# Attention, a layer-normed MLP and a token-and-channel mixer on one core: the same instructions, with the SBUF tiles placed in another order

## The chip, the cores and the metric

The kernel runs on one core of a Trainium2 chip. The time is the device time of one launch in microseconds (us). Three runs of the kernel before took 1301.6, 1305.14 and 1305.99 us; the median is 1305.14 us.

## The reference

Three stages follow each other. B = 4 batches, H = 12 heads, S = 448 positions, D = 64 per head, C = 768 channels, all in float32:

```python
scores = cap * np.tanh((q @ k.T / 8) / cap)            # per batch and head, 448 x 448
attn   = softmax(scores, axis=-1)
x      = concat_heads(attn @ v)                        # (4, 448, 768)

xn = (x - mean) / np.sqrt(var + 1e-6) * g_ln
x  = x + np.maximum(xn @ w_ch1, 0) @ w_ch2             # 768 -> 3072 -> 768

h  = np.maximum(x.transpose(0, 2, 1) @ w_tok1, 0) @ w_tok2   # 448 -> 256 -> 448
u  = x + h.transpose(0, 2, 1)
out = u + np.maximum(u @ m2_w_ch1, 0) @ m2_w_ch2       # 768 -> 1536 -> 768
```

## The kernel before

Activations stay in SBUF with the channels on the partitions: a batch is six tiles of 128 channels by 448 positions. A large matrix product is done in float32r, in one pass of TensorE, and its accuracy is kept by splitting each operand into a high part and a low remainder (`low`, line 183): a product of two split operands is three matmuls (`PASSES`: high by high, low weight by high, high weight by low). Nearly every matmul so made reads 128 partitions by 128 columns as weights and then lets 128 by 448 move through them (128 by 384 in the first half of the token mixing).

The stages, by lines: attention of batches 0 and 1 with plain float32 matmuls (L467, L488), of batches 2 and 3 with split operands (L470, L513); the MLP layers of batches 0 and 1 (`mlp`: L1025 first layer, L998 second layer); token mixing (`tokens`: transposes L1059, products L1083 and L1108); for batches 2 and 3 the layers' products go through a seven-product (Strassen) form, all of whose matmuls are issued at L782. Weights come from HBM in 64-bit words, are put together on ScalarE and VectorE, split, and written back to HBM so that a later use only loads them. Attention of batches 2 and 3 runs beside the MLP of 0 and 1.

The order in which every engine gets its instructions is set by `Program.emit`, a list scheduler with a table of costs of its own. It runs while the kernel is built and knows nothing of addresses.

What concerns the change is where the tiles lie. All SBUF tiles come from one pool (`cp`) through `place` (line 173) and `boxes` (line 176). The pool hands out bytes of a partition in the order of the calls, and each tile begins at the next multiple of 32 bytes. The first tile, `kc`, begins at byte 16,512 of each partition and takes 704, so what follows begins at 17,216, which is 269 times 64. Which tiles a matmul reads as weights and which move:

- weights: `split0` to `split2` (weights of the layers), `whole` (whose room becomes `late_whole`, a fourth set), `t1` (first token matrix), `ks` and `vs` (keys and values of split attention), `pair_r`, `ones`;
- moving: `big0`, `big1` (normalised activations, split), `h0` to `h7` (hidden activations, split), `x0` to `x3`, `raw`, `own`, `two`, `qs`, `eh`, `el` and `t2`; the rooms of `x0`, `x1`, `raw`, `own` and `two` hold split operands too in the Strassen stages (`late_x`, `late_raw`, ...).

Within a tile the parts that a matmul reads begin at multiples of 512 bytes (weights; 640 in `vs`) or of 1792 and 1536 bytes (moving), which are all multiples of 64. So the place of a tile's first byte modulo 64 is that of every read from it.

Of the kernel before, what the change touches and what calls it, by code (L numbers as in the profile page):

```python
# [10 lines left out]
F32R = mybir.dt.float32r  # L11
I32 = mybir.dt.int32
U32 = mybir.dt.uint32
I64 = mybir.dt.int64
# [4 lines left out]
B, H, S, D = 4, 12, 448, 64  # L19
C = H * D  # L20
P = 128
NCC = C // P
# [3 lines left out]
G = 4  # L26
NG1, NG2 = NF1 // G, NF2 // G
NG = NG1 + NG2
DT = 256
NJ = S // 32  # L30
# [3 lines left out]
DV = D + 32  # L34
# [58 lines left out]
class Program:  # L93
# [12 lines left out]
    def add(self, engine, cols, run, reads=(), writes=(), early=0.0, lag=None, slack=0.0):  # L106

        names = [(name.strip("*+"), "*" in name, "+" in name) for name in engine.split("/")]  # L110
        costs = {e: self.FIXED[e] + self.RATE[e] * cols * (0.5 if half else 1.0) for e, half, _ in names}
        step = Step(costs, run, (self.key - early, len(self.steps)))
        step.port = {e for e, _, port in names if port}
        step.lag, step.slack = lag, slack
        before = set()
        for b in [p for b in reads for p in b.parts]:
            before.add(b.writer)
            b.readers.append(step)
        for b in [p for b in writes for p in b.parts]:
            before.add(b.writer)  # L120
            before.update(b.readers)
            b.writer, b.readers = step, []
        before -= {None, step}
        for s in before:
            s.users.append(step)
        step.waits = len(before)
        self.steps.append(step)
# [36 lines left out]
def block_kernel(ctx: ExitStack, tc: tile.TileContext, qkv, cap, gln, w1, w2, wt1, wt2, con, out):  # L164
# [10 lines left out]
    def place(name, shape, dtype=F32, tag=""):  # L175
        return cp.tile([P, *shape], dtype, name=name, tag=tag or name)

    def boxes(name, n, shape, dtype=F32):
        return [Box(place(f"{name}{i}", shape, dtype)) for i in range(n)]
# [11 lines left out]


    kc = place("kc", [K_PAIR])
    cap_t, tsc = place("cap_t", [1]), place("tsc", [1])
    gl = place("gl", [NCC])
    ones = place("ones", [P])
    pair_r = place("pair_r", [3, P], F32R)
    t1, t2 = place("t1", [2, 4 * DT], F32R), place("t2", [2, 2 * S], F32R)
    T1 = [Box(t1[:, :, i * 512:(i + 1) * 512]) for i in range(2)]
    T2 = [Box(t2[:, :, i * S:(i + 1) * S]) for i in range(2)]  # L200
    ident = kc[:, K_ID:K_ID + P]
    neg = kc[:, K_NEG:K_NEG + 1]

    raw_t, whole_t = place("raw", [2 * C], I64), place("whole", [2 * C], I32)
    RAW, WHOLE = [[Box(t[:, i * C:(i + 1) * C]) for i in range(2)] for t in (raw_t, whole_t)]
    split_t = [place(f"split{i}", [2, C], F32R) for i in range(3)]
    SPLIT = [[Box(t[:, :, :CC]), Box(t[:, :, CC:])] for t in split_t]
    x_t = [place(f"x{b}", [NCC, S]) for b in range(B)]
    X = [[Box(t[:, e]) for e in range(NCC)] for t in x_t]
    big_t = [place(f"big{i}", [NCC, 2, S], F32R) for i in range(2)]  # L210
    BIG = [[Box(t[:, e]) for e in range(NCC)] for t in big_t]
    HID = boxes("h", 2 * G, [2, S], F32R)


    own_t = place("own", [4, S])
    own = [Box(own_t[:, i]) for i in range(4)]
    own[2].parts = [Box(), Box()]
    OWN = [Box(own_t[:, 2 * i:2 * i + 2], own[2 * i:2 * i + 2]) for i in range(2)]
    QK = boxes("qk", 1, [S + 4 * P])
    QK[0].parts = [Box(QK[0].at[:, :S + 2 * P]), Box(QK[0].at[:, S + 2 * P:])]  # L220
    v_t, two_t = place("v", [4 * DV]), place("two", [2, S])
    V = [Box(v_t.rearrange("p (c d) -> p c d", c=4))]
    two = [Box(two_t[:, i]) for i in range(2)]
    SQ, SUM, OTHER = boxes("sq", 1, [S]), boxes("sum", 1, [S]), boxes("other", 1, [S])
    TWICE = [Box(OTHER[0].at[:, :CC].rearrange("p (e a d) -> p e a d", e=3, a=2), OTHER)]
    QS = boxes("qs", 1, [2, S], F32R)
    KS, VS = boxes("ks", 1, [4 * P], F32R), boxes("vs", 1, [4, DV + D], F32R)
    EH, EL = boxes("eh", 1, [2, S], F32R), boxes("el", 1, [2, S], F32R)
    M, N = boxes("m", 2, [2, 2, NJ]), boxes("n", 1, [2, 2, NJ])
    rs_t, rm_t = place("rs", [H, NJ]), place("rm", [H, NJ])  # L230
    RS = [Box(rs_t[:, 6 * g:6 * g + 6]) for g in range(2)]
    RM = [Box(rm_t[:, 6 * g:6 * g + 6]) for g in range(2)]
    R, VA = boxes("r", 1, [2, 32]), boxes("va", 1, [3, 8])
# [9 lines left out]
    def ring(of):  # L243
        while True:
            yield from of
# [6 lines left out]
    H11, H21, H4 = BIG[1][:2], [BIG[1][2], TWO], [*EH, *EL]  # L252
    H22, H1, H2, H3 = (HID[i:i + 2] for i in range(0, 8, 2))

    def relay():

        def later(old, boxes, fill):
            old = [p for box in old for p in box.parts]
            add("place", 0, fill, (), old + boxes)
# [9 lines left out]
        def fill_raw():  # L269
            t = place("late_raw", [3, 2, S], F32R, tag="raw")  # L270
            for i in range(3):
                X3[i].at = t[:, i]
            X4[2].at = QS[0].at

        later(RAW + QS, [*X3, X4[2]], fill_raw)

# [151 lines left out]
    def attention(b, start, pace):  # L428
# [8 lines left out]
        def head(h):  # L437
# [10 lines left out]
            if parted:  # L448

                (ks,), (qs,) = KS, QS  # L450
                add("act", 4 * P, lambda: act(ks.at, k, AF.Copy), [qk], [ks], early=PREPARE)  # L451
# [213 lines left out]

    HIDDEN = [ring(HID), ring(HID[:G]), ring(HID[G:])]
    PASSES = ((0, 0), (1, 0), (0, 1))
# [575 lines left out]
```

## Time and profile before

| | |
|---|---|
| median of 3 runs | 1305.14 us (1301.6 to 1305.99) |
| profiled execution: span from first to last instruction (the page gives no other time of it) | 1303.0 us |
| PE busy | 1289.0 us, 99%, 6171 matmuls |
| PE weight loads | 1115.8 us, 86%, 6171 |
| VectorE (DVE) busy | 1119.3 us, 86% |
| ScalarE (ACT) busy | 759.9 us, 58% |
| mean DMA rate | 210 GB/s |
| mean granted TensorE clock | 0.999 |

A matmul's busy time runs from its start to the end of its last result. Matmuls overlap, so the mean time of one (367 ns) is not the time from one to the next; the latter is read from a row that merges n matmuls of the chain of waits, by dividing its length by n. A float32 matmul that isn't a transpose stands as two records, a float32r matmul as one. All 6171 records that the program's matmuls should leave are there; 5597 of them are float32r, and of these 5412 move 448 columns in the lines L998, L1025, L782, L470, L513, L1108 and L574, and 176 move 384 columns in L1083.

### The profile page before, as it was taken

Reading aid. Unit: us, or ns where it says so; the run is one execution under the profiler, and the core shown is the slowest. Engines: PE = TensorE matmul, PEld = TensorE weight load, DVE = VectorE, ACT = ScalarE, POOL = GpSimd, SP = SyncE. Lnnn points to the kernel's source line nnn. Section 1 sums busy time; section 2 is a strip of 40 time slices with the busy share of each in tenths; the row PEclk is TensorE's granted clock in tenths of the full one; section 3 lists DMA queues with packets and bytes.
Section 4 is the critical chain, followed back from the end, with each engine's and each line's share of the span. In section 5 each row is a group of like instructions: output and inputs, shape, how many; then the busy total and the mean of one; then the engine's idle time right before and its main releaser. Section 6 shows DMA issues by size and latency. Waiting matters only on the chain.

```text
span 1303.0 us, 17972 instructions
## 1 busy us (share of the span) xinstructions
PE 1289.0 (99%) x6171; PEld 1115.8 (86%) x6171; DVE 1119.3 (86%) x1997; ACT 759.9 (58%) x1225; POOL 114.6 (9%) x89
## 2 busy tenths in 40 slices
PE   9999999999999999999999999999999999999998
PEld 4435589999999999989899998899999999988997
DVE  5889699999999999899956788878879889797877
ACT  8987668687866578687533434542443533573442
POOL 2330002020110012120000001200000000010000
PEclk9999999999999999999999999999999999999999
DMA  8888447977878786755868676655554454036453
GB/s 311 303 286 294 146 168 264 314 222 270 277 260 280 242 279 231 245 187 201 306 215 304 226 221 201 168 165 156 158 170 141 140 167 155 19 102 176 150 167 127
DMA packets 155226, 273.96 MB, mean 210 GB/s; under 512 B 11520, under 2 KB 109312, under 8 KB 155136
## 3 DMA queue, kind: packets, MB, share of 16 engines
q1 hardware_dynamic: 152256, 269.40, 62.7%
q0 software_dynamic: 2304, 3.15, 1.6%
q8 instruction: 48, 0.79, 0.2%
q10 hardware_dynamic: 576, 0.29, 0.1%
q14 instruction: 42, 0.34, 0.1%
HBM read 182.35 MB, written 90.44 MB: 209 GB/s over the span
## 4 chain that ended last, share of the span: by engine, by line
PE 75%; DVE 4%; DMA 2%; ACT 1%; issue 1%; POOL 0%; DVEq 0%; ACTq 0%
PE late_bank L782 18%; PE bank L1025 17%; PE bank L998 17%; PE bank L782 13%; PE sc L470 2%; PE bank L513 2%; PE bank L1083 2%; PE bank L1108 2%; PE late_bank L1083 1%; DMA raw<-in_w 1%; PE late_bank L1108 1%; DMA split<-keeps 0%; DMA late_vs<-wholes 0%; PE bank L1059 0%; DVE h L184 0%
## 5 line engine op out<-in xcount | busy, mean ns | idle before, releaser
L998 PE MATMUL bank<-h,split 128*128 128x448 f32 x1296 | 276.6, 367 | 2.2 <-DVE x L1002 1.1
L1025 PE MATMUL bank<-big,split 128*128 128x448 f32 x1296 | 277.0, 368 | 0.3 <-DVE big L184 0.2
L1025 PEld LDWEIGHTS bank<-big,split 128*128 128x128 f32 x1296 | 242.2, 188 | 24.9 <-issue 3.1
L998 PEld LDWEIGHTS bank<-h,split 128*128 128x128 f32 x1296 | 242.4, 188 | 24.2 <-DVE x L1002 2.4
L349 ACT ACTIVATE whole<-raw 128x512 f32<-128x512 f32 (+2 forms) x94 | 70.8, 754 | 27.5 <-DVE split L184 17.1
L782 PE MATMUL late_bank<-big,split 128*128 128x448 f32 x378 | 84.0, 366 | 0.6 <-DVE other L769 0.6
L1030 ACT ACTIVATE h<-bank 128x448 fp32r<-128x448 f32 x72 | 38.9, 541 | 69.3 <-PE bank L1025 68.9
L1002 DVE TENSOR_TENSOR x<-x,bank 128x448 f32<-128x448 f32 x108 | 66.0, 611 | 14.8 <-PE bank L998 14.3
L782 PEld LDWEIGHTS late_bank<-big,split 128*128 128x128 f32 x378 | 70.8, 188 | 7.0 <-DVE other L769 1.0
L188 ACT ACTIVATE split<-whole 128x512 fp32r<-128x512 f32 (+1 forms) x63 | 44.5, 707 | 53.4 <-PE bank L998 36.2
L352 ACT ACTIVATE raw<-raw 128x512 int32<-128x512 uint32 (+2 forms) x94 | 71.1, 757 | 0.1
L184 DVE TENSOR_TENSOR split<-whole,split 128x512 fp32r<-128x512 f32 (+1 forms) x80 | 63.9, 800 | 7.3 <-ACT split L188 6.9
L184 POOL TENSOR_TENSOR ks<-qk,ks 64x512 fp32r<-64x512 f32 x24 | 34.5, 1439 | 397.9 <-ACT ks L451 368.6
L769 DVE TENSOR_TENSOR x<-bank,x 128x448 f32<-128x448 f32 x106 | 63.6, 617 | 6.1 <-PE bank L782 5.9
L358 DVE CUSTOM_DVE_ANT_0 whole<-raw,whole 128x1024 uint16<-128x1024 uint16 (+2 forms) x84 | 67.0, 798 | 1.5
L478 DVE TRANSPOSE_TENSOR_REDUCE m<-x 128x28 f32<-128x896 f32 x48 | 52.0, 1097 | 10.5 <-ACT x L474 10.2
L1031 DVE SCALAR_TENSOR_TENSOR h<-bank,h 128x448 fp32r<-128x448 f32 x72 | 44.3, 616 | 15.7 <-ACT h L1030 15.5
L782 PE MATMUL bank<-h,split 128*128 128x448 f32 x240 | 54.8, 367 | 1.0 <-DVE split L184 0.9
L478 DVE TRANSPOSE_TENSOR_REDUCE m<-own 128x28 f32<-128x896 f32 x48 | 52.6, 1096 | 2.6 <-ACT own L474 2.6
L769 DVE TENSOR_TENSOR x<-late_bank,x 128x448 f32<-128x448 f32 x82 | 49.9, 617 | 5.3 <-PE late_bank L782 5.1
L526 DVE TRANSPOSE_TENSOR_REDUCE n<-own 128x28 f32<-128x896 f32 x48 | 52.7, 1098 | 0.1
L473 ACT ACTIVATE own<-sc,tsc 128x896 f32<-128x896 f32 x48 | 48.0, 1002 | 7.8 <-DVE x L535 4.6
(488 smaller groups left out, 2674.2 us busy)
## 6 DMA issues: line engine op xcount, KB each, us to landing
split<-kept SPq DMA_DIRECT2D x73, 384.0 KB, 4.0
raw<-in_w SPq DMA_DIRECT2D x36, 768.0 KB, 6.1
kept<-split SPq DMA_DIRECT2D x36, 768.0 KB, 4.2
raw<-in_w SPq DMA_DIRECT2D x54, 512.0 KB, 4.7
keeps<-split SPq DMA_DIRECT2D x54, 512.0 KB, 3.9
split<-keeps SPq DMA_DIRECT2D x44, 384.0 KB, 4.0
qk<-in_qkv SPq DMA_DIRECT2D x33, 480.0 KB, 4.0
whole<-whole SPq DMA_DIRECT2D x36, 384.0 KB, 3.2
```

The lines of the kernel that those rows point to most:

```text
L184: eng.tensor_tensor(out, whole, high.bitcast(F32), op=ALU.subtract)
L349: add("act", m * 1.1, lambda: act(f.bitcast(F32), hi.bitcast(F32), AF.Prelu, scale=2.0 ** -112, alpha=2.0 ** 32), [r], [w])
L352: act(lo, lo.bitcast(U32), AF.Copy, scale=2.0 ** -29)
L358: add("pool+" if ahead else "dve+", m, lambda e: engine_of[e].tensor_tensor(f, f, lo, op=ALU.add), [r], [w])
L473: add("act", 2 * S + 94, lambda e=e, sc=sc: act(e, sc.at[:, :, :S], AF.Tanh, scale=tsc), [sc], eb)
L478: add("dve", 2 * S, lambda half=half, e=e: dve.tensor_reduce(m.at[:, half].rearrange("p c j -> p (c j)"), e.rearrange("p c (j i) -> p (c j ...
L526: add("dve", 2 * S, lambda half=half, e=e: dve.tensor_reduce(n.at[:, half].rearrange("p c j -> p (c j)"), e.rearrange("p c (j i) -> p (c j ...
L769: add("dve", S, lambda: dve.tensor_tensor(to.at, bank.at[:, :S], t.at, op=ALU.add), [bank, t], [to], early=FIRST)
L782: mm(bank.at[:, :S], w(wi), x.at[:, xi], start=first and (i, n) == (0, 0), stop=(i, n) == (len(parts) - 1, 2), skip_group_check=not first)
L998: mm(py.at[:, :S], w[:, wi, i * P:(i + 1) * P], h[i].at[:, hi], start=(i, n) == (0, 0), stop=(i, n) == (G - 1, 2))
L1002: add("dve", S, lambda x=x, py=py: dve.tensor_tensor(x.at, x.at, py.at[:, :S], op=ALU.add), [py], [x], early=EVACUATE)
L1025: mm(ph.at[:, :S], w[:, wi, cc * P:(cc + 1) * P], src[cc].at[:, xi], start=(cc, n) == (0, 0), stop=(cc, n) == (NCC - 1, 2))
```

## The change

The calls that place the tiles stand in another order. First come the tiles that matmuls read as weights, then `cap_t` and `tsc`, which take 32 bytes each and so 64 together, then the tiles that move, then the rest (`qk0`, `v`, `gl` and the small ones). `gl`, which takes 32 bytes, no longer stands ahead of the large tiles.

```diff
     kc = place("kc", [K_PAIR])
-    cap_t, tsc = place("cap_t", [1]), place("tsc", [1])
-    gl = place("gl", [NCC])
     ones = place("ones", [P])
     pair_r = place("pair_r", [3, P], F32R)
-    t1, t2 = place("t1", [2, 4 * DT], F32R), place("t2", [2, 2 * S], F32R)
+    t1 = place("t1", [2, 4 * DT], F32R)
+    split_t = [place(f"split{i}", [2, C], F32R) for i in range(3)]
+    whole_t = place("whole", [2 * C], I32)
+    KS, VS = boxes("ks", 1, [4 * P], F32R), boxes("vs", 1, [4, DV + D], F32R)
+    cap_t, tsc = place("cap_t", [1]), place("tsc", [1])
+
+    raw_t = place("raw", [2 * C], I64)
+    x_t = [place(f"x{b}", [NCC, S]) for b in range(B)]
+    big_t = [place(f"big{i}", [NCC, 2, S], F32R) for i in range(2)]
+    HID = boxes("h", 2 * G, [2, S], F32R)
+    own_t, two_t = place("own", [4, S]), place("two", [2, S])
+    QS = boxes("qs", 1, [2, S], F32R)
+    EH, EL = boxes("eh", 1, [2, S], F32R), boxes("el", 1, [2, S], F32R)
+    rs_t, rm_t = place("rs", [H, NJ]), place("rm", [H, NJ])
+    t2 = place("t2", [2, 2 * S], F32R)
...
-    v_t, two_t = place("v", [4 * DV]), place("two", [2, S])
+    v_t, gl = place("v", [4 * DV]), place("gl", [NCC])
...
-    QS = boxes("qs", 1, [2, S], F32R)
-    KS, VS = boxes("ks", 1, [4 * P], F32R), boxes("vs", 1, [4, DV + D], F32R)
-    EH, EL = boxes("eh", 1, [2, S], F32R), boxes("el", 1, [2, S], F32R)
...
-    rs_t, rm_t = place("rs", [H, NJ]), place("rm", [H, NJ])
```

Where the tiles begin, as the byte in the partition and its remainder by 64 and by 128:

| tile | read as | before | by 64, 128 | after | by 64, 128 |
|---|---|---|---|---|---|
| `split0` | weights | 53,152 | 32, 32 | 27,456 | 0, 64 |
| `whole` | weights | 47,008 | 32, 32 | 45,888 | 0, 64 |
| `t1` | weights | 19,360 | 32, 32 | 19,264 | 0, 64 |
| `ks0` | weights | 211,360 | 32, 32 | 52,032 | 0, 64 |
| `big0` | moving | 114,592 | 32, 32 | 112,000 | 0, 0 |
| `h0` | moving | 157,600 | 32, 32 | 155,008 | 0, 0 |
| `x0` | moving | 71,584 | 32, 32 | 68,992 | 0, 0 |
| `el0` | moving | 219,552 | 32, 32 | 201,600 | 0, 0 |

The other tiles of the two lists above go with their kind, but for `t2` (before 32 by 64, after 0 by 64 and 64 by 128). Before, all of them begin 32 bytes past a multiple of 128. After, all begin at a multiple of 64, the weights at an odd one and what moves at an even one. Every engine has the same instructions in the same order with the same waits; only addresses differ, so no rows of an order are shown.

## Rows read from the trace of the kernel before

**Rows 1.** The page: busy time and share of each engine.
```profile
PE 1289.0 (99%) x6171; PEld 1115.8 (86%) x6171; DVE 1119.3 (86%) x1997; ACT 759.9 (58%) x1225; POOL 114.6 (9%) x89
```

**Rows 2.** The page: who ended last, share of the span by engine.
```profile
PE 75%; DVE 4%; DMA 2%; ACT 1%; issue 1%; POOL 0%; DVEq 0%; ACTq 0%
```

**Rows 3.** Stretches: busy us (instructions) of PE, PEld, DVE, ACT, POOL; clock, DMA share, GB/s.
```profile
200.00:300.00 100.00, 99.90 (x494) 91.91 (x493) 96.40 (x159) 76.52 (x113) 16.80 (x12) 1.00 0.82 268
300.00:400.00 100.00, 100.00 (x493) 91.97 (x492) 96.73 (x153) 76.14 (x107) 15.26 (x11) 1.00 0.79 271
400.00:500.00 100.00, 100.00 (x493) 91.40 (x492) 92.24 (x166) 65.27 (x100) 8.96 (x7) 1.00 0.78 259
...
840.00:1100.00 260.00, 260.00 (x1285) 240.93 (x1284) 220.57 (x427) 108.10 (x209) 0.00 (x0) 1.00 0.50 156
1130.00:1300.00 170.00, 168.06 (x817) 152.01 (x815) 143.16 (x273) 76.01 (x150) 6.99 (x8) 1.00 0.47 136
```

**Rows 4.** Chain of waits, in order of time: start us, length us, what ran.
```profile
325.94 6.20 PE bank L1025 x30
...
648.40 29.19 PE bank L1025 x144
677.59 29.18 PE bank L998 x144
...
1058.55 10.94 PE late_bank L782 x54
```

**Rows 5.** Chain of waits from 1100 us on: 384-column matmuls, then the last stage.
```profile
1110.53 3.84 PE bank L1083 x22
...
1195.00 5.58 PE late_bank L782 x27
...
1263.82 9.30 PE late_bank L782 x45
```

**Rows 6.** Groups from 39.6 to 41.3 us: a float32 matmul's records (busy us, mean ns).
```profile
L488 PE MATMUL bank<-x,x 128*96 128x448 f32 x3 | 1.3, 537 | 0.0
```

**Rows 7.** Timeline of the same stretch: start us, length us.
```profile
40.19 1.29 PE L488 MATMUL bank<-x,x 128*96 128x448 f32 x3
```

**Rows 8.** Groups by form on PE, over the span: busy us, mean ns, idle before.
```profile
L1025 PE MATMUL bank<-big,split 128*128 128x448 f32 x1296 | 277.0, 368 | 0.3 <-DVE big L184 0.2
L998 PE MATMUL bank<-h,split 128*128 128x448 f32 x1296 | 276.6, 367 | 2.2 <-DVE x L1002 1.1 <-DMA split<-keeps 1.1
```

**Rows 9.** Groups by form of the weight loads, over the span.
```profile
L998 PEld LDWEIGHTS bank<-h,split 128*128 128x128 f32 x1296 | 242.4, 188 | 24.2 <-DVE x L1002 2.4 <-issue 1.1 <-DVE late_own L184 0.9
```

**Rows 10.** The longest waits of PE: us in total, times, longest.
```profile
PE bank L1108 <- DVE h L1064: 1.7, 2, 0.9
PE sc L467 <- ACT x L473: 1.7, 2, 1.4
PE bank L998 <- DVE x L1002: 1.1, 1, 1.1
```

More of the change, by code (lines that the diff above doesn't have):

```diff
@@ L202, in block_kernel @@
     neg = kc[:, K_NEG:K_NEG + 1]
-    raw_t, whole_t = place("raw", [2 * C], I64), place("whole", [2 * C], I32)
     RAW, WHOLE = [[Box(t[:, i * C:(i + 1) * C]) for i in range(2)] for t in (raw_t, whole_t)]
-    split_t = [place(f"split{i}", [2, C], F32R) for i in range(3)]
     SPLIT = [[Box(t[:, :, :CC]), Box(t[:, :, CC:])] for t in split_t]
-    x_t = [place(f"x{b}", [NCC, S]) for b in range(B)]
     X = [[Box(t[:, e]) for e in range(NCC)] for t in x_t]
-    big_t = [place(f"big{i}", [NCC, 2, S], F32R) for i in range(2)]
     BIG = [[Box(t[:, e]) for e in range(NCC)] for t in big_t]
-    HID = boxes("h", 2 * G, [2, S], F32R)
-    own_t = place("own", [4, S])
     own = [Box(own_t[:, i]) for i in range(4)]
```

## The prediction

> **What bounds the kernel now.** I read the page's busy shares first. PE is busy 99% of the span and nothing else is above 86% [rows 1]. The chain of what ended last then gives PE 75% of the span, against 4% for VectorE and 2% for DMA [rows 2]. PE's own waits add up to little: the three longest are 1.7, 1.7 and 1.1 us [rows 10]. In the table of stretches PE is busy for 99.9 to 100 us of each 100 between 200 and 500 us, at the full granted clock of 2.4 GHz (the upper of its two levels) [rows 3]. So PE's stream of matmuls is the bound, and a change that removes no instruction and no wait can only act through the time from one matmul's start to the next. A change of addresses would have to show there.
>
> That step can be read from pieces of the chain that hold nothing but equal matmuls. 144 matmuls of L1025 take 29.19 us, 144 of L998 take 29.18, 54 of L782 take 10.94 [rows 4]: 202.7 ns each in all three. Other pieces give a second step: 30 in 6.20 us [rows 4], 27 in 5.58 and 45 in 9.30 [rows 5], each 206.7 ns. Which of the two holds seems not to depend on line or tile: L1025 has 206.7 at 326 us and 202.7 at 648, and L782 has 202.7 at 1058 and 206.7 at 1264, with one granted clock throughout [rows 3 to 5]. A step lasts for long stretches, as if it were fixed when the stream restarts after a break.
>
> At 2.4 GHz 448 columns are 186.7 ns, so the shorter step holds 16.0 ns that are no columns. The 384-column matmuls take 3.84 us for 22, 174.5 ns against 160.0, so 14.5 over [rows 5]. Float32 matmuls don't have this. A record there makes 448 columns in two passes: three records last 1.29 us, and taking off the 537 ns of the last leaves 0.753 us for two steps, 376.5 ns against 373.3, 3 ns over [rows 6, 7]. Float32 takes an element of SBUF every second cycle, float32r one in every cycle. What costs the 13 ns between them thus shows only where the operand is read at twice the rate, and it is somewhat smaller for the shorter operand. I take it for a cost of reading, though a cost of exchanging float32r weights isn't excluded: the weight loads last 188 ns beside each of these matmuls [rows 9].
>
> **The change part by part.** Instructions, their order and their waits stay. So nothing is queued behind anything new, no DMA is moved or made larger, and SP's and POOL's queues are as they were; these parts cost nothing and need no cover. What changes is where reads begin. Before, each float32r matmul read both operands from 32 bytes past a multiple of 64; after, it reads both from a multiple of 64. No float32r matmul of the kernel before reads from such a place, so the trace prices the change only from both sides.
>
> One side is nothing: 0 ns. The other is all that float32r pays over float32, 16.0 less 3, 13 ns. Between them lies a countable loss. If the reader takes SBUF in blocks of 64 bytes (16 columns, 16 / 2.4 GHz = 6.7 ns), 1792 bytes from a multiple of 64 are 28 blocks, and from 32 past it 29, of which half the first and half the last are wasted. One whole block would be 6.7 ns; if the rest of a last block costs nothing since the next operand may begin, half a block, 3.3 ns. The rows show no such block; they show two steps 4.0 ns apart (206.7 less 202.7), so the stream does shift by amounts of this size. I take 3.3 ns as it is the price nearest to that difference, and keep 0 and 13 for the range. Below nothing there is a bound as well: a stream may settle on the longer step, 4.0 ns worse.
>
> The count is the 1296 + 1296 of L1025 and L998 [rows 8] and those of the other float32r lines, 5412 with 448 columns in all, and 176 with 384. The sum: 5588 x 3.3 ns = 18.6 us (half of 6.67 ns, unrounded). All of it lies on the path only if the feeders keep up. VectorE is nearest to its limit: it is idle for 3.6 us of the stretch from 200 to 300 us and for 3.3 us of the next [rows 3]. The 494 matmuls of such a stretch give back 1.6 us, so it remains covered; at 6.7 ns they give 3.3, just as much as there is, and at 13 ns 6.4, of which about 3 would turn into waits in each of the two stretches. From 840 us on VectorE has 39 us free in 260, and nothing is late next.
>
> The profiled execution's span is 1303.0 us, 2.1 below the median of the runs, which include it. I set the sum against the median: 1305.1 less 18.6 is 1286.5 us.
>
> A rule of the Trainium skill speaks against it. "SBUF — State Buffer" (its table "Specifications (TRN2)") gives SBUF lines of 16 bytes. By that rule a shift of 32 is two whole lines, every read touches as many lines as before, and the time stays at 1305; the trace, in which all these reads share one remainder, neither bears it out nor denies it. It is the first rival below.
>
> **The rivals.** First, no change. Placing does nothing, or the step shifts by so little that it can't be told. For it: the step is the same for L1025, L998 and L782 [rows 4], which read other tiles from end to end of SBUF, so addresses in the large play no part. Against it: what they all share is just the remainder that changes. The time is 1305, and about 1302 if the last stage comes to run at the shorter step (its 817 matmuls [rows 3] x 4.0 ns = 3.3 us).
>
> Second, the whole 13 ns go. For it: float32 shows that the engine can do with 3 ns over [rows 6, 7]. Against it: 13 ns is more than one block, so a misplaced start explains only part. 5412 x 13 ns are 70 us and 176 x 11.5 another 2; less the 6 that VectorE holds back at 200 to 400 us, 66 us, so 1239. The Trainium skill's "TensorE: Matmul & The Clock Gate" (section "Back-to-back issue gap") gives N / 2.4 + 2.5 ns, for 448 columns 189.2 ns; the trace's 202.7 disagrees for float32r, and at 189.2 ns the 5412 would save 73 us.
>
> Third, slower: the stream settles on the longer step. It is one mechanism, on PE, wherever the stream restarts after a break; the price is 4.0 ns for each matmul until the next restart. For it: the last stage ran so throughout, and did not return to 202.7 [rows 5]. That weights and moving operands now differ by 64 bytes modulo 128 could make it more frequent, if both are read from the same part of the memory at the same time. Against it: both steps occur with one and the same placement. It decides the sign from about 1000 more matmuls at the longer step on (1000 x 4.0 ns = 4.0 us, 0.3%). If all 4595 others take it, it costs 18.4 us: 1323.
>
> **How the numbers follow.** About 0.3% (3.9 us) is what the measurement can tell from no change; the runs before span 4.4 us. I give the forecast, reads from multiples of 64 cost a few ns less, 0.38; no change 0.36; the whole cost gone 0.08; slower 0.18. Faster is 0.38 + 0.08 = 0.46, same 0.36, slower 0.18. The forecast's own range is from a whole block (5588 x 6.7 ns = 37 us, 1268) with a little below it to the edge of no change: 1262 to 1301. The range for 8 in 10 has to hold no change and most of the slower case too; I leave out about 0.06 below and 0.10 above: 1240 to 1312.
>
> **What would show it.** If the forecast is right, the chain's long pieces of L1025, L998 and L782 are shorter for the same count: 144 in about 28.7 us (199.4 ns), and in the last stage 45 in fewer than 9.30. The 22 of L1083 shrink by about as much per matmul (174.5 to 171), the records of L488 not at all (376.5), and PE's waits and the other engines' mean times stay. If pieces still read 29.19 us for 144, placement does nothing. If they read 27.3, the whole cost was one of placement. If they read 29.8 for 144 where they read 29.2, the longer step has spread. The forecast is wrong in kind if the time falls or rises while PE's step stays at 202.7 and 206.7 in the same stretches: then something other than PE's reads depends on the place, such as ScalarE or VectorE (their mean times would tell) or DMA.

## The result, and the profile after

The changed kernel takes 1287.41 us (median of 4 runs, 1286.77 to 1287.65), the kernel before 1303.37 (4 runs, 1300.98 to 1305.99). The ratio is 0.9873, 95% interval 0.9852 to 0.9895: 1.3% faster. With its fourth run the kernel before has a median 1.8 us under the 1305.14 that the forecast started from. Beside two of the later experiments, e5_pads64 and e6_gap192, the changed kernel was timed once more as **e7_after**:

> The changed kernel once more, beside the others on the same chip: 1286 to 1289 us.

It took 1287.71 us, ratio 0.9879 (0.9859 to 0.9899).

The page of after has the shares of [rows 1] to within one point; PE loses 19.1 us of busy time, VectorE 1.2 and ScalarE 1.6:

```profile
span 1284.9 us, 17972 instructions
PE 1269.9 (99%) x6171; PEld 1112.8 (87%) x6171; DVE 1118.1 (87%) x1997; ACT 758.3 (59%) x1225; POOL 114.8 (9%) x89
```

The span fell by 18.1 us, and PE's stream is where it went. In after the chain of waits leaves part of the middle unnamed, so the counterpart of [rows 4] is read from PE's timeline (start, length, what ran). Such a row is longer than its steps by the drain, the time for which its last matmul outlasts a step, so the step is taken from start to start:

```profile
668.65 28.96 PE L1000 MATMUL bank<-h,split 128*128 128x448 f32 x144
697.45 28.96 PE L1027 MATMUL bank<-big,split 128*128 128x448 f32 x144
726.25 14.56 PE L1000 MATMUL bank<-h,split 128*128 128x448 f32 x72
```

144 matmuls take 28.80 us, 200.0 ns each, where [rows 4] had 202.7. The drain is 0.16 us (28.96 less 28.80); it serves again below. For the last stage the chain stands as in [rows 5]:

```profile
1180.34 5.40 PE late_bank L784 x27
...
1246.94 9.00 PE late_bank L784 x45
```

27 in 5.40 and 45 in 9.00 us are 200.0 ns, where [rows 5] had 206.7. The longer of the two steps isn't to be seen in any of these pieces any more. 18.1 us over 5412 matmuls are 3.3 ns each, between the 2.7 ns that a matmul at the shorter step gains and the 6.7 of one at the longer, as it has to be when both steps stood before.

The feeders still keep up. In the two stretches where VectorE was nearest to its limit [rows 3] its idle time shrank from 3.6 and 3.3 us to 2.7 and 1.5:

```profile
200.00:300.00 100.00, 99.47 (x499) 92.55 (x498) 97.34 (x160) 77.03 (x114) 17.04 (x12) 1.00 0.83 275
300.00:400.00 100.00, 100.00 (x503) 93.59 (x502) 98.53 (x158) 75.89 (x108) 15.25 (x11) 1.00 0.79 276
```

PE's longest waits are the first two of [rows 10], no longer in total:

```profile
PE bank L1110 <- DVE h L1066: 1.6, 2, 1.0
PE sc L469 <- ACT x L475: 1.4, 1, 1.4
```

The third of [rows 10] has 1.3 us, 0.2 more than before.

### The profile page after: what moved, and what is told of

Its sections match the earlier page's. It is cut to its first block, busy times and chain, and to the rows that moved or that the text cites. A ratio compares the mean times of both kernels' runs of the same rounds, so it can differ in the third digit from the quotient of the medians.

```text
span 1284.9 us, 17972 instructions
## 1 busy us (share of the span) xinstructions
PE 1269.9 (99%) x6171; PEld 1112.8 (87%) x6171; DVE 1118.1 (87%) x1997; ACT 758.3 (59%) x1225; POOL 114.8 (9%) x89
## 5 line engine op out<-in xcount | busy, mean ns | idle before, releaser
L1000 PE MATMUL bank<-h,split 128*128 128x448 f32 x1296 | 272.3, 364 | 1.8 <-DVE x L1004 1.3
L1027 PE MATMUL bank<-big,split 128*128 128x448 f32 x1296 | 272.5, 364 | 0.4 <-DVE big L184 0.3
L784 PE MATMUL bank<-h,split 128*128 128x448 f32 x240 | 53.8, 363 | 1.2 <-DVE split L184 1.1
```

The source lines that it names most:

```text
L784: mm(bank.at[:, :S], w(wi), x.at[:, xi], start=first and (i, n) == (0, 0), stop=(i, n) == (len(parts) - 1, 2), skip_group_check=not first)
L1000: mm(py.at[:, :S], w[:, wi, i * P:(i + 1) * P], h[i].at[:, hi], start=(i, n) == (0, 0), stop=(i, n) == (G - 1, 2))
L1027: mm(ph.at[:, :S], w[:, wi, cc * P:(cc + 1) * P], src[cc].at[:, xi], start=(cc, n) == (0, 0), stop=(cc, n) == (NCC - 1, 2))
```

## The experiments

After the result two theories stood, one of them in two forms. A: a read that begins at a multiple of 64 bytes is shorter (the forecast); A1 says so of the moving operand alone, A2 of the weights alone. C: only the distance counts, which is how many bytes behind its weights the moving operand begins; before, it was 0, and the change made it 64 bytes modulo 128.

**e1_pad32** aligns all tiles and keeps the order.

```diff
     gl = place("gl", [NCC])
+    place("pad", [8])
     ones = place("ones", [P])
```

> The order of before, with one empty tile of 32 bytes ahead of the large tiles, so that all of them begin at a multiple of 64 (and at 64 modulo 128, weights and moving operands alike). Theory A (a read that begins at a multiple of 64 is what counts): the whole gain, 1286 to 1290 us, and a step of 200.0 ns in pieces of equal matmuls. Theory C (the 64 bytes modulo 128 between weights and moving operands count): no gain, 1301 to 1306 us and steps of 202.7 and 206.7 ns.

Measured: 1303.0 us, ratio 1.0018 (0.9998 to 1.0037), no gain. The chain of waits has the step of before, 202.7 ns:

```profile
647.01 29.19 PE bank L1026 x144
```

A is refuted, and with it the mechanism of the forecast.

**e2_nogap** keeps the order of after and its multiples of 64, but takes the 64 bytes away.

```diff
-    cap_t, tsc = place("cap_t", [1]), place("tsc", [1])
-
     raw_t = place("raw", [2 * C], I64)
...
     v_t, gl = place("v", [4 * DV]), place("gl", [NCC])
+    cap_t, tsc = place("cap_t", [1]), place("tsc", [1])
```

> The order of after, but cap_t and tsc placed behind the moving tiles, so that weights and moving operands both begin at 64 modulo 128 and no 64 bytes part them. Theory A: as after, 1286 to 1290 us, step 200.0 ns. Theory C: as before, 1301 to 1306 us.

Measured: 1301.51 us, ratio 1.0001 (0.9982 to 1.0021). Neither order nor alignment did anything: the gain is the 64 bytes. The chain of waits:

```profile
645.41 29.76 PE bank L1026 x144
...
1261.89 9.12 PE late_bank L783 x45
```

Here the stretch at 645 us has 206.7 ns and the last stage 202.7, the reverse of [rows 4, 5] at the same distance, 0. So which of the two steps holds isn't tied to a place in the program.

**e3_mv32 and e4_w32** move one kind of operand off the multiple of 64.

```diff
     cap_t, tsc = place("cap_t", [1]), place("tsc", [1])
+    place("pad", [8])
     raw_t = place("raw", [2 * C], I64)
```

e4_w32 has such a line there and one more ahead of `ones`; so it moves all the moving tiles by 64 bytes and the weights by 32.

> The order of after with 32 empty bytes ahead of the moving tiles: weights begin at a multiple of 64, what moves 32 past one. Theory A1 (the moving operand's start counts): 1300 to 1306 us, steps of 202.7 or 206.7 ns. Theory A2 (the weights' start counts): 1286 to 1290 us, 200.0 ns. If both count in parts, between 1290 and 1300.

> The order of after with 32 empty bytes ahead of the weights and 32 ahead of the moving tiles: weights begin 32 past a multiple of 64, what moves at a multiple of 64. Theory A1 (the moving operand's start counts): 1286 to 1290 us, step 200.0 ns. Theory A2 (the weights' start counts): 1300 to 1306 us, 202.7 or 206.7 ns.

Measured: e3_mv32 1311.09 us, ratio 1.0071 (1.005 to 1.0092); e4_w32 1310.37, ratio 1.0065 (1.0042 to 1.0087). Both are slower than before, which neither A1 nor A2 allows. In both what moves lies 96 bytes behind the weights, and both chains of waits have one and the same step, 205.3 ns; first e3_mv32, then e4_w32:

```profile
650.33 29.57 PE bank L1027 x144
```

```profile
648.66 29.57 PE bank L1028 x144
```

**m1_probe** adds rows of 40 equal matmuls behind the last work of after, in this form, each with its own starts and columns:

```diff
         prog.emit()
+        bk, mv, wt = BANKS[0].at, big_t[0].rearrange("p e a s -> p (e a s)"), split_t[0].rearrange("p a c -> p (a c)")
+        for _ in range(40): mm(bk[:128, :448], wt[:, 0:128], mv[:, 8:456], start=True, stop=True)  # mv 32 B
```

> After, with 17 rows of 40 equal float32r matmuls added behind its last work, on one PSUM bank; each row has its own start of the moving operand and of the weights, and its own number of columns. Steps in ns. Theory A1 (a 64-byte block of the moving operand): 448 columns from 0 and from 64 bytes 200.0, from 4, 16, 32 and 48 bytes 202.7 or 206.7 all alike, weights moved by 32 or 64 bytes alone 200.0. Theory of finer lines (16 bytes): 16, 32 and 48 as 0, only 4 longer. Theory A2 (weights): the rows with weights moved by 32 bytes are longer. What lies over the columns at an aligned start: if it is a fixed exchange of weights, 512, 448, 384 and 256 columns are each 13.3 ns over their columns (226.7, 200.0, 173.3, 120.0); if it grows with the bytes read, 15.2, 13.3, 11.4 and 7.6 ns. With 64 columns of weights a fixed exchange may shrink; a cost of the moving read stays.

Rows of PE's timeline; a row's step is its length less 0.16 us, by 40. L1205 is aligned, L1206 has the moving start 4 bytes on, L1208 32 bytes on, L1210 64 bytes, L1211 the weights 32 on, L1212 both 32 on, L1213 the weights 64 on; L1214, L1216 and L1218 are aligned with 512, 384 and 256 columns, and L1220 is aligned with 64 columns of weights:

```profile
1281.64 8.16 PE L1205 MATMUL bank<-big,split 128*128 128x448 f32 x40
1289.65 8.43 PE L1206 MATMUL bank<-big,split 128*128 128x448 f32 x40
...
1306.04 8.37 PE L1208 MATMUL bank<-big,split 128*128 128x448 f32 x40
...
1322.52 8.32 PE L1210 MATMUL bank<-big,split 128*128 128x448 f32 x40
1330.67 8.42 PE L1211 MATMUL bank<-big,split 128*128 128x448 f32 x40
1338.93 8.16 PE L1212 MATMUL bank<-big,split 128*128 128x448 f32 x40
1346.93 8.27 PE L1213 MATMUL bank<-big,split 128*128 128x448 f32 x40
1355.04 9.33 PE L1214 MATMUL bank<-big,split 128*128 128x512 f32 x40
...
1373.55 7.10 PE L1216 MATMUL bank<-big,split 128*128 128x384 f32 x40
...
1387.55 4.87 PE L1218 MATMUL bank<-big,split 128*128 128x256 f32 x40
...
1397.05 8.21 PE L1220 MATMUL bank<-big,split 128*64 128x448 f32 x40
```

200 ns where nothing is moved and again where both are moved by 32; 205 and 204 where only the moving start is (by 32 and 64); 206 and 203 where only the weights' start is. So it is the distance of the two operands, and either's own place is nothing. Half the columns of weights don't make the step shorter (201). At the same distance, 64, the rows of 256, 384 and 512 columns take 117.8, 173.5 and 229.2 ns, which is 11.1, 13.5 and 15.9 over their columns, beside 13.3 for 448. That is neither of the two that were expected, a fixed cost (13.3 for each) or one in proportion to the bytes (7.6, 11.4 and 15.2).

**m2_probe** moves one start on in steps of 64 bytes, alternates starts, and tries plain float32.

> After, with 21 rows of equal matmuls added behind its last work. Theory C (while a matmul streams, the next one's weights are read, and the two reads hinder each other by their distance modulo 128 bytes). Sixteen rows move the operand on by 64 bytes each from 0 to 960: by C every even row (0, 128, 256 ...; 64 modulo 128 from the weights) has about 200 ns, every odd row 203 to 207; if a longer period counts, the even rows differ among themselves. Two rows alternate between two starts: in one each matmul's own weights lie 64 modulo 128 from what moves, but the next matmul's weights 0; in the other the reverse. By C, which looks at the next weights, the first has 203 to 207 ns and the second 200; if a matmul's own weights counted, 200 and 203 to 207. Three rows of plain float32, which moves a column every second cycle: by C, if full rate is what makes the two reads collide, 375 to 377 ns from one record to the next at all three starts (0, 64 and 32 bytes).

The first five of sixteen rows (0 to 256 bytes), then the two alternating rows and one of float32 (20 records, 0.54 us of which are the last one's own time):

```profile
1283.45 8.16 PE L1205 MATMUL bank<-big,split 128*128 128x448 f32 x40
1291.45 8.32 PE L1206 MATMUL bank<-big,split 128*128 128x448 f32 x40
1299.61 8.25 PE L1207 MATMUL bank<-big,split 128*128 128x448 f32 x40
1307.70 8.27 PE L1208 MATMUL bank<-big,split 128*128 128x448 f32 x40
1315.80 8.16 PE L1209 MATMUL bank<-big,split 128*128 128x448 f32 x40
...
1412.84 8.17 PE L1221 MATMUL bank<-big,split 128*128 128x448 f32 x40
1420.84 8.27 PE L1222 MATMUL bank<-big,split 128*128 128x448 f32 x40
1428.95 7.68 PE L1223 MATMUL bank<-big,split 128*128 128x448 f32 x20
```

200, 204, 202, 203 and again 200: the period is 256 bytes, not the 128 of the theory, and the eleven other rows of this kind repeat it to 0.01 us. Float32 has (7.68 less 0.54) / 19 = 375.8 ns at all three starts (0, 64 and 32 bytes on); it doesn't feel the distance. The alternating rows came out against C's idea of the next weights: the step is 200 where a matmul's own weights lie 64 from what moves (L1221), and 203 where the next one's do (L1222).

**e5_pads64** parts most tiles of the two kinds by 64 bytes within the order of before.

```diff
+    place("pad_x", [16])
     x_t = [place(f"x{b}", [NCC, S]) for b in range(B)]
...
+    place("pad_k", [16])
     KS, VS = boxes("ks", 1, [4 * P], F32R), boxes("vs", 1, [4, DV + D], F32R)
+    place("pad_e", [16])
     EH, EL = boxes("eh", 1, [2, S], F32R), boxes("el", 1, [2, S], F32R)
```

> The order of before, in which every operand begins 32 past a multiple of 64; only three empty tiles of 64 bytes are put in, so that what moves lies 64 modulo 128 from what is read as weights (but for raw's room, some 160 matmuls). Theory C: nearly all of the gain, 1286 to 1291 us, step 200 ns. If a start at a multiple of 64 were needed as well: 1300 to 1306 us.

Measured: 1289.73 us, ratio 0.9896 (0.9874 to 0.9919). Three empty tiles give nearly the whole gain, with every operand still 32 past a multiple of 64 and the order as it was. From start to start in PE's timeline 144 take 28.80 us again:

```profile
670.66 28.96 PE L1001 MATMUL bank<-h,split 128*128 128x448 f32 x144
699.46 28.96 PE L1028 MATMUL bank<-big,split 128*128 128x448 f32 x144
```

The tiles that the pads don't part show the cause within this one kernel. `raw`'s room stays at distance 0 from `late_whole`, and nine matmuls on the two take 206.7 ns each (2.02 us less the drain), among neighbours at 200; in after, at 64, the same nine take 200.0. First e5_pads64, then after:

```profile
847.69 2.02 PE L785 MATMUL bank<-late_raw,late_whole 128*128 128x448 f32 x9
```

```profile
845.25 1.96 PE L784 MATMUL bank<-late_raw,late_whole 128*128 128x448 f32 x9
```

Such pairs, and others that the pads leave 192 bytes apart modulo 256 (`qs` and `ks`), fit the 2.0 us by which e5_pads64 lies above e7_after.

**e6_gap192** puts 192 bytes between the two kinds.

```diff
     cap_t, tsc = place("cap_t", [1]), place("tsc", [1])
+    place("pad", [32])
     raw_t = place("raw", [2 * C], I64)
```

> The order of after with 192 bytes instead of 64 between weights and moving tiles, the same modulo 128 and another modulo 256. Theory C with a period of 128: as after, within 0.2%. If modulo 256 counts, some tenths of a per cent either way, and m2_probe's even rows show which.

Measured: 1296.57 us, ratio 0.9947 (0.9927 to 0.9967), 0.7% above after. The chain of waits has 202.2 ns, as m2_probe's row for that distance (L1207):

```profile
643.80 29.12 PE bank L1027 x144
```

So 128 isn't the period in the kernel either: 192 is 64 modulo 128, and the kernel has the step of the row for 192, not that for 64.

**m3_probe** fills in distances, turns through three starts, and has other numbers of columns.

> After, with 17 rows of equal matmuls added behind its last work. m2_probe gave a period of 256 bytes: 200.0 ns where what moves begins 64 bytes behind its weights modulo 256, 203.9, 202.2 and 202.8 at 128, 192 and 0. Eleven rows fill in other distances (144, 160, 176, 208, 224, 240, 16, 32 and 48 bytes behind, and 8 bytes to either side of 64). If the 64-byte block counts alone, all lie between 200 and 204; from m1_probe (203 to 207 for parts of 64) I expect 203 to 207, and none under 200. Three rows turn through three starts, so that what moves lies 64 behind its own weights, behind the next matmul's, or behind those of the one after; in each row the other two relations are others than 64. The row with 200 ns names the weights that are read beside a matmul's stream: own (as the two alternating rows of m2_probe would have it), or two ahead, which they could not tell from it. The theory that I held before, the next one's, would have 200 in the second row and 202 to 204 in the others. Three rows have 256, 384 and 512 columns at distance 0 modulo 256: if the loss comes with the load of weights and not with the columns, each is 2.8 ns over the aligned ones (117.8, 173.35, 228.9).

L1206 lies 160 bytes behind, L1212 32, L1214 72, L1215 56; L1216 to L1218 are the three turning rows (own, next, second next); L1219 to L1221 have 256, 384 and 512 columns at distance 0:

```profile
1290.75 8.17 PE L1206 MATMUL bank<-big,split 128*128 128x448 f32 x40
...
1339.48 8.42 PE L1212 MATMUL bank<-big,split 128*128 128x448 f32 x40
...
1355.85 8.43 PE L1214 MATMUL bank<-big,split 128*128 128x448 f32 x40
1364.11 8.17 PE L1215 MATMUL bank<-big,split 128*128 128x448 f32 x40
1372.12 8.78 PE L1216 MATMUL bank<-big,split 128*128 128x448 f32 x42
1380.74 8.57 PE L1217 MATMUL bank<-big,split 128*128 128x448 f32 x42
1389.15 8.61 PE L1218 MATMUL bank<-big,split 128*128 128x448 f32 x42
1397.59 4.95 PE L1219 MATMUL bank<-big,split 128*128 128x256 f32 x40
1402.38 7.10 PE L1220 MATMUL bank<-big,split 128*128 128x384 f32 x40
1409.32 9.27 PE L1221 MATMUL bank<-big,split 128*128 128x512 f32 x40
```

By the three probes together, the step for 448 columns where what moves begins so many bytes behind its weights modulo 256:

| bytes | 0 | 16 | 32 | 48 | 56 | 64 | 72 | 80 | 96 | 112 | 128 | 144 | 160 | 176 | 192 | 208 | 224 | 240 |
|---|---|---|---|---|---|---|---|---|---|---|---|---|---|---|---|---|---|---|
| ns | 203 | 202 | 206 | 203 | 200 | 200 | 207 | 203 | 205 | 207 | 204 | 206 | 200 | 204 | 202 | 204 | 204 | 203 |

No simple rule of blocks gives this, and none lies under 200. The distances 0 and 32 were each reached in two ways, by moving the weights and by moving the other operand, with rows of the same length (8.27 us for L1213 of m1_probe and L1208 of m2_probe; 8.42 for L1211 of m1_probe and L1212 here). The turning rows contradict the alternating ones: now own weights at 64 give 205 ns, the next one's 200 and those after 201. So the runs do not name one pair of reads that hinder each other, and this stays open. The rows with other columns refute what I expected of them: at distance 0, 256, 384 and 512 columns take 119.8, 173.5 and 227.8 ns. Beside m1_probe's rows at distance 64, 256 columns lose 2.0 ns by distance 0, 384 nothing, 448 lose 2.7, and 512 gain 1.5. So which of the two distances is the better hangs on the number of columns.

**e8_gap160 and e9_gap288** carry the table to the kernel at two more distances, with a pad of 24 and of 56 elements where e6_gap192 has 32.

> The order of after with 96 empty bytes more ahead of the moving tiles, so that they lie 160 bytes behind the weights modulo 256 instead of 64, and begin 32 past a multiple of 64. If the table of steps by distance modulo 256 that the added rows gave holds in the kernel: 200.0 ns (as for 64), 1286 to 1290 us. If 64 modulo 128 is needed: 1300 us or more.

> The order of after with 224 empty bytes more, so that what moves lies 288 bytes (32 modulo 256) behind the weights. By the table of the added rows 206.7 ns for 448 columns, 6.7 more than after: 5412 x 6.7 ns = 36 us, 1318 to 1326 us. If only 64-byte blocks matter: 1300 to 1306 us.

Measured: e8_gap160 1293.08 us, ratio 0.9914 (0.9887 to 0.9941); e9_gap288 1306.9, ratio 1.0032 (1.001 to 1.0054). Both missed the range, as each of these two distances has a second step. Their chains of waits, e8_gap160 first:

```profile
640.86 29.75 PE bank L1027 x144
...
1252.63 9.00 PE late_bank L784 x45
```

```profile
647.61 29.75 PE bank L1027 x144
...
1267.86 9.00 PE late_bank L784 x45
```

206.6 ns in the one stretch and 200.0 in the other, in both. A row of the probes catches one of the two steps, and a kernel, in which many separate stretches follow each other, takes both; so a value of the table is one step of its distance, and another may exist. Among the distances that were run as kernels (0, 32, 64, 96, 160 and 192) only 64 keeps to one short step; 96 and 192 keep to one as well, but a longer one (205.3 and 202.2). No version beats after.

## Why the prediction was right or wrong

The time and the sign were right: 1286.5 us forecast, 1287.4 measured. The fall was forecast as 18.6 us; the spans fell by 18.1 and the medians by 16.0 (1303.4 to 1287.4), so the time came out nearer than the fall because the forecast started from 1305.1; that much of the agreement is luck. The reason given was wrong.

- **PE's step is the bound, and a change of place must show there**: right. All of it came from the step, and waits and other engines stayed.
- **The step that failed is "If the reader takes SBUF in blocks of 64 bytes ..."**, the price of a start that isn't a multiple of 64. The runs put that price at nothing: 1.0018 (0.9998 to 1.0037) with alignment alone (e1_pad32), and nearly the full gain without it (e5_pads64). What the 3.3 ns per matmul are instead is the distance between the operands: 202.7 or 206.7 ns at 0 became 200.0 at 64. That the two figures agree is chance, and so is it that 64 bytes stand in both: the forecast's 64 is a place to begin at, and what acted are the 64 bytes of `cap_t` and `tsc` between the two kinds.
- **The bounds**: float32's 3 ns over its columns was taken as what float32r might come to. The lowest step that any run showed in a row of 448 is 200.0, 13.3 ns over the columns; at 256, 384 and 512 columns the lowest are 11.1, 13.5 and 14.4 over. So no place that was tried takes away most of the 16.0 ns; what that remainder is, the runs don't show. "Somewhat smaller for the shorter operand" was read from 16.0 against 14.5; at distance 64 the two lengths pay nearly the same, 13.3 and 13.5, and in the added rows distance 0 costs 448 columns 2.7 ns more and 384 nothing, so the difference was the distance at work.
- **384 columns**: forecast 171, but the added rows have 173.5 at distance 64 as well as at 0 (7.10 us for 40). Only 176 matmuls of the kernel have 384 columns, so it is little.
- **First rival, no change**: by the rule of 16-byte lines that "SBUF — State Buffer" of the Trainium skill gives (its table "Specifications (TRN2)"), a shift of both operands by 32 bytes is nothing. e1_pad32 agrees (1.0018). The rule doesn't speak of two operands' distance, and there the change acted.
- **Third rival, slower**: it named what counts, the distance of the two reads, as a reason for the longer step, and had the sign wrong for the 64 bytes of the change. At 96 bytes (e3_mv32, e4_w32) the kernel is slower, by 0.7%, but by one step of its own, 205.3 ns, and not by a longer stay at 206.7.

In plain words: each float32r matmul has weights and a moving operand to read, and the time to the next matmul hangs on the distance of the two starts modulo 256 bytes. Shown are that dependence, its period for 448 columns, that moving both operands together does nothing, and that plain float32 doesn't have it at the three starts that were tried. That two reads hinder each other in the memory is a reading that fits, but no run shows it, and which weights would meet which stream isn't settled. The Trainium skill ("TensorE: Matmul & The Clock Gate", section "Step-by-step: what each phase is for") has the weights and the moving operand on two independent read ports, so that loading weights takes nothing from a running matmul. By that rule the distance could do nothing, and the time would have stayed near 1303 us; 200.0 against 206.7 ns for the same matmuls disagrees for float32r.

## What to carry to other kernels

Where float32r matmuls run back to back, read the step from a long piece of equal matmuls, and try the distance between the weights' and the moving tiles modulo 256 bytes before any reordering: 64 bytes between them were worth 1.3% here (1.0% as three empty tiles in the old order), and 96 cost 0.7%. Try it with the kernel's own number of columns: 64 bytes beat 0 for 448 columns, and lost to it for 512 in the added rows. If long pieces of one kernel show two steps, a placement with one step is to be looked for in the whole kernel and not only in a row of equal matmuls. A forecast whose size fits can still have the wrong cause; the two runs that told them apart were the alignment without the distance (e1_pad32) and the distance without the alignment (e5_pads64).

## What the runs showed of the hardware that was not expected

- A matmul of float32r has two stable steps at some distances (202.7 and 206.7 ns at 0, in [rows 3 to 5] at one granted clock; 200.0 and 206.6 at 160 and at 32), and a stretch keeps the one that it has fallen into. At 64 only 200.0 was seen in the long pieces of 448 columns, and the runs of after spread by 0.9 us where those of before spread by 5.
- The distance works to a few bytes: 56 and 64 have 200 ns, 68 and 72 have 207.
- Of the 13.3 ns that remain over 448 columns, half the columns of weights (64) take nothing away (201 ns, at distance 64).
